# Network two with seven-product steps: four output sums placed singly at the hand-over between passes, weight stores and loads at other slots, last joins on VectorE

## The chip, the cores and the metric

The kernel runs on one core of a Trainium2 chip. The metric is the time of one execution on the device in microseconds (us); less is better. PE is TensorE (matrix products), DVE is VectorE, ACT is ScalarE, POOL is GpSimd, and SP is the queue that issues nearly all DMAs.

## What is computed

Three stages follow each other on 4 x 3072 = 12288 tokens of 256 values, all in float32:

```python
X = np.fft.fft(np.fft.fft(x, axis=1), axis=2).real
xk = mu_k * X + (1.0 - mu_k) * x_prev          # x_prev: the token before
xr = mu_r * X + (1.0 - mu_r) * x_prev
k = np.maximum(xk @ w_k, 0.0)                  # 256 -> 1024
y = 1.0 / (1.0 + np.exp(-(xr @ w_r))) * ((k * k) @ w_v)
h = y @ w_in                                   # 256 -> 2048
out = (h - np.tanh(h)) @ w_out                 # 2048 -> 256
```

The last two lines are network two, the part that the change concerns.

## The kernel before

**Number format.** Every float32 operand of a product is held as two tiles, a rounded high part (cast by ACT, `hi`) and the rest (subtracted by DVE or POOL, `lo`). One product is three matmuls (`mm3`, lines 395 to 397 in the trace): high x high, high x low, low x high. Each moves 512 columns.

**Passes and steps.** The tokens go through in 12 passes of 2 x 512. Network one takes 4 quads of a pass, network two 8 steps, each with 256 of the 2048 hidden units. A step (n, q) is one 2 x 2 block product: the first matrix by seven products after Winograd (`P`), tanh and subtraction on the four blocks, then the second matrix. The four sums of a pass that leave the core are the PSUM tiles `o` (in the code `C[n, t, h]`, t the token half, h the channel half). In pass 0 and in odd steps the second matrix takes eight products that go straight into `o` (`whole`). In even steps of passes 1 to 11 it takes seven (hence "sevens"): three go straight into `o` (`direct`: a12, s4, a22), four go to a bank `k` and are added up in SBUF tiles `acc` (`apart`: a11, s2, s3, s1), since each of them enters several outputs. PE does the second matrix of a step one or two steps later, so the last products of pass n-1 fall into steps (n, 0) and (n, 1).

**The turn.** When pass n-1 is done, `joined` forms the four sums of the `acc` tiles with four additions, in step (n, 0), and `ready` adds each of them to its `o` tile on DVE and issues the store of 256 KB. Both calls of `ready` stand in step (n, 1), and each handles two outputs one behind the other. Ten turns (n = 2 to 11) are of this kind; the turn from pass 0 to pass 1 has no `acc` tiles, and `done` copies the four `o` tiles out.

**What sets the order.** The program is written out by hand: every engine runs its instructions in the order of the code, and waits stand only where data or a buffer are missing. Besides, `at(slot, f)` puts jobs into numbered slots, and each call of `fill()` runs the jobs of one slot. A step has four slots; z0 = 192 is the slot of step (0, 0).

**Weights of network two.** `weights2(slot, q)` loads a block of `w_in` from the DRAM buffer `wf` (line 926), splits it and forms its sums into the tile `TI` (`ti`, ACT and POOL), and four slots later forms the rest (`TI<-t`). `keep` (line 940) stores the finished tile to the DRAM buffer `ti`, from which `stream` (line 1190) reads it back three steps ahead of use in passes 1 to 11. `seven(slot, q)` does the same for the block of `w_out` that an even step needs (`W7`, three loads at line 951, two slots ahead of the first use). The loads of both for the seven-product forms share the one buffer `wf` of pool `p2a`. `left2` loads the next pass's inputs (`xk<-spill`) and forms their sums on POOL.

**Names in the rows.** `x`, `z`, `w`, `k` are PSUM banks of one step, `c` a tanh, `g` a block of h - tanh(h), `m`, `a`, `s` its high and low parts for whole, a and s products. Line 1138 is the addition `z<-w,s` on DVE that frees `w` for the next product; line 1145 subtracts the tanh; line 1068 is ACT's copy `z<-x` at the head of a step, on which PE adds a12.

Of the kernel before, what the change touches and what calls it, by code (L numbers as in the profile page):

```python
# [406 lines left out]
class Kernel:  # L407
# [513 lines left out]
    def weights2(self, slot, q, pool, tag, bufs):  # L921
# [17 lines left out]
        def keep():  # L939
            self.nc.sync.dma_start(out=self.ti[q], in_=out[0].rearrange("p s k n -> p (s k n)").bitcast(F32))  # L940
        self.at(slot, load(a, self.p2a, "wf", 1, 4 + q), ti, None, None, None, lambda: b[0](None))
        self.at(16 * NP + ((5, 6, 10)[q] if q < 3 else 4 * q - 3), keep)
        self.at(slot + 4, load(b, pool, tag, bufs, 12 + q), None, wo)

    def seven(self, slot, q):

        src, t, i = [], [], q // 2
        def load():
            src.append(self.p2a.tile([128, TOK], F32, tag="wf", name="wf", bufs=1) if q else self.kp.tile([128, TOK], F32, tag="xt", name="wf", bufs=4))
            for to, at, n in ((0, 128, 128), (128, 0, 128), (256, 256, 256)):  # L950
                self.nc.sync.dma_start(out=src[0][:, to:to + n], in_=self.wf[12 + q, :, at:at + n])
        def first():
            self.W7[q] = self.p2a.tile([128, 2, 7, 128], F32R, tag=f"TI{i}", name="W7")
            f, g = self.quad_weights(self.p2b, self.W7[q])
            f(src[0])
            t.append(g)
        self.at(slot, load, None, first, None, None, None, lambda: t[0](None))

# [21 lines left out]
    def whole(self, p, blk):  # L980
# [4 lines left out]
        if p["n"] == 0:  # L985
            return self.second(p, blk)
        c = p["w"][int(blk[1]) - 1]
# [30 lines left out]

    def joined(self, n):

        G = self.G
        s1, s2, s3, s5 = (self.acc[n, k] for k in ("a11", "s2", "s3", "s1"))
        G.tensor_add(s2, s2, s1)
        G.tensor_add(s3, s3, s2)
        G.tensor_add(s2, s2, s5)
        G.tensor_add(s5, s5, s3)

    def ready(self, p, t):

        n = p["n"]  # L1030
        if n == 0:
            return
        for h, k in enumerate((("a11", "s2"), ("s3", "s1"))[t]):
            a = self.acc.pop((n, k))
            self.V.tensor_add(a, a, self.C.pop((n, t, h)))
            self.nc.sync.dma_start(out=self.out[n, t, :, h], in_=a)

    def step(self, n, q):
# [30 lines left out]
        if seven:  # L1069
# [6 lines left out]
            P(X, "s2")  # L1076
            late("l12")
            s2 = copied(X)
            t11 = bend(Z)
# [8 lines left out]
            lo("a11", g, G)  # L1088
            add()
            self.fill()  # L1090
            Wb = self.bank("w", "w")
# [6 lines left out]
            if p2 and q == 0:  # L1098
                self.joined(n - 1)
            self.direct(p2, "s4")  # L1100
# [9 lines left out]
        else:  # L1110
# [4 lines left out]
            P(X, "s2")  # L1115
            late("ls1")
            s2 = copied(X)
            t11 = bend(Z)
# [12 lines left out]
            late("hs2", "+s4", "ls2")  # L1131
            if q == 1:
                self.ready(p2, 1)
            self.fill()
# [4 lines left out]
            t22 = bend(Z)  # L1139
            late("hs4", "ls4")  # L1140
            self.fill()
            add()
            if q > 1:
                self.direct(p1, "a12")
            V.tensor_sub(Z, Z, t22)
            hi("22", Z)
            if q == 1:
                self.ready(p2, 0)
            lo("22", Z, V)
# [29 lines left out]
    def phase2(self):  # L1179
# [12 lines left out]
        for g in range(8, 8 * NP):  # L1192
            self.at(z0 + 4 * (g - 3) + 2, lambda g=g: stream(g))
        self.TI = dict(enumerate(self.TI))
        for n in range(NP):
            for q in range(8):
                if n == 0 and q == 1:
                    self.xctx.close()
                    self.p2b = self.ctx.enter_context(self.tc.tile_pool(name="p2b", bufs=1, side="right", reuse_waits="tile"))
                    for j in range(3, 8):  # L1200
                        self.weights2(z0 + 4 * (j - 2), j, self.kp, "xt", 4)
                    for j, slot in ((0, 18), (2, 25), (4, 36), (6, 44)):
                        self.seven(z0 + slot, j)
                if q == 1 and n + 1 < NP:
                    u = self.left2(n + 1)
                    if n == 0:
                        self.at(z0 + 10, u["load"], None, u["a11"], None, u["a12"], None, u["a22"], u["+s1"], u["+s3"], u["+s2"], u["+s4"],
                                u["s1"], None, u["s3"], None, u["s2"], None, u["s4"])
# [8 lines left out]
            if n == 0:  # L1217
                self.pend["over"] = set()
        p, w = self.pend, self.older
        late = lambda *names: [p["late"][k]() for k in names]  # L1220
        late("t21", "c12", "g21", "t12", "h21", "g12", "l21", "h12", "l12")
        self.whole(p, "11")
        add = self.apart(w, "s3")
        self.whole(p, "22")
        add()
        self.direct(w, "s4")
        add = self.apart(w, "s2")
        add()
        self.joined(NP - 1)
        self.whole(p, "21")  # L1230
        self.ready(p, 1)
        self.whole(p, "12")
        self.ready(p, 0)


# [106 lines left out]
```

## Time and profile before

| | us |
|---|---|
| median of 3 runs | 1650.86 (1649.0 to 1650.99) |
| the profiled execution | 1649.88 |
| its span, first to last instruction | 1648.1 |
| PE busy | 1606.5 (97%) |
| DVE, ACT, POOL busy | 1309.6, 1194.2, 1101.5 |
| mean granted TensorE clock | 0.995 of full |

The spectrum takes the first 110 us, network one lasts to 645 us, network two from there to the end. A row of the timeline gives the start, the duration, the engine, the line, the operation with its tiles, and in brackets the idle time of that engine just before it with what ended it. Matmuls are pipelined: a row of 0.39 us starts about 0.23 us behind the one before.

### The profile page before, as it was taken

How to read it: one execution, taken by the hardware profiler on the slowest of the kernel's cores; microseconds unless marked ns; L12 is line 12 of the kernel's file. 1: busy time of each engine (PE TensorE's matmuls, PEld its weight loads, DVE VectorE, ACT ScalarE, POOL GpSimd, SP SyncE). 2: the span in 40 equal slices, each digit the busy share in tenths (PEclk: the TensorE clock that was granted, in tenths of full speed). 3: DMA queues.
4: the chain of work that ended last, by engine and by line, in shares of the span. 5: the costliest groups of instructions: out<-in, count | busy, mean ns of one | idle time of the engine just before them, and what ended most of it. 6: DMA issues, size and time to landing. Idle time of an engine off the chain costs nothing.

```text
span 1648.1 us, 22348 instructions
## 1 busy us (share of the span) xinstructions
PE 1606.5 (97%) x7346; PEld 1322.0 (80%) x7346; DVE 1309.6 (79%) x2023; ACT 1194.2 (72%) x2289; POOL 1101.5 (67%) x913
## 2 busy tenths in 40 slices
PE   8999999999999999989999999999999999999997
PEld 7978888888888887767778787878787878787876
DVE  7987888888898897657777777777777777777776
ACT  5887777777777777767767777777777777777764
POOL 1166667666666666577777768686868686868654
PEclk9999999999999999989999999999999999999999
DMA  9620111011111121544242424242424242414130
GB/s 336 174 58 27 46 46 65 20 45 58 46 65 63 47 90 51 202 156 173 86 139 97 141 90 141 90 141 90 141 90 141 90 146 85 161 69 163 68 116 26
DMA packets 58341, 167.96 MB, mean 102 GB/s; under 512 B 6753, under 2 KB 14945, under 8 KB 58225
## 3 DMA queue, kind: packets, MB, share of 16 engines
q1 hardware_dynamic: 56640, 162.08, 28.6%
q0 software_dynamic: 1440, 4.46, 1.6%
q8 instruction: 58, 0.95, 0.2%
q14 instruction: 59, 0.48, 0.1%
q10 hardware_dynamic: 144, 0.00, 0.0%
HBM read 127.65 MB, written 38.86 MB: 101 GB/s over the span
## 4 chain that ended last, share of the span: by engine, by line
PE 85%; DVE 5%; POOL 3%; ACT 2%; issue 2%; DMA 2%; SPq 1%; POOLq 0%; DVEq 0%; ACTq 0%
PE o L396 11%; PE o L397 11%; PE o L395 11%; PE x L395 7%; PE x L396 7%; PE x L397 7%; PE w L395 4%; PE w L396 4%; PE w L397 4%; PE k L395 2%; PE k L397 2%; PE k L396 2%; PE z L395 2%; PE z L397 2%; PE z L396 2%
## 5 line engine op out<-in xcount | busy, mean ns | idle before, releaser
L1060 POOL TENSOR_TENSOR a<-g,a 128x512 fp32r<-128x512 f32 x132 | 170.4, 1291 | 138.5 <-ACT a L1058 138.0
L696 POOL TENSOR_TENSOR a<-xk,a 128x512 fp32r<-128x512 f32 x70 | 93.2, 1334 | 123.1 <-ACT a L694 123.1
L1060 POOL TENSOR_TENSOR s<-g,s 128x512 fp32r<-128x512 f32 x132 | 170.4, 1295 | 1.0
L395 PE MATMUL o<-m,WO 128*128 128x512 f32 x416 | 162.5, 391 | 0.0
L397 PE MATMUL o<-m,WO 128*128 128x512 f32 x416 | 162.4, 390 | 0.0
L396 PE MATMUL o<-m,WO 128*128 128x512 f32 x416 | 162.4, 390 | 0.0
L696 POOL TENSOR_TENSOR s<-xk,s 128x512 fp32r<-128x512 f32 x94 | 124.8, 1328 | 39.5 <-ACT s L694 36.1
L396 PE MATMUL o<-m,wv 128*128 128x512 f32 x384 | 149.6, 390 | 0.1
L397 PE MATMUL o<-m,wv 128*128 128x512 f32 x384 | 149.5, 389 | 0.0
L395 PE MATMUL o<-m,wv 128*128 128x512 f32 x384 | 149.5, 389 | 0.0
L1050 ACT ACTIVATE c<-z 128x512 f32<-128x512 f32 x176 | 106.6, 606 | 53.2 <-DVE z L1094 31.5
L1167 POOL TENSOR_TENSOR g<-g,g 128x512 f32<-128x512 f32 x88 | 114.0, 1296 | 45.6 <-DVE x L1166 34.7
L1058 ACT CAST a<-g 128x512 fp32r<-128x512 f32 x132 | 82.4, 624 | 58.9 <-DVE g L1104 30.9
L1054 ACT COPY s<-x 128x512 f32<-128x512 f32 x176 | 103.6, 588 | 27.7 <-PE x L397 26.6
L1016 DVE TENSOR_TENSOR acc<-acc,k 128x512 f32<-128x512 f32 x132 | 90.7, 687 | 21.7 <-PE k L397 21.3
L571 ACT ACTIVATE c<-z 128x512 f32<-128x512 f32 x112 | 67.2, 600 | 55.1 <-DVE z L660 54.1
L578 DVE TENSOR_TENSOR m<-z,m 128x512 fp32r<-128x512 f32 x112 | 76.8, 686 | 35.4 <-ACT m L576 35.4
L1058 ACT CAST s<-g 128x512 fp32r<-128x512 f32 x132 | 82.0, 621 | 17.2 <-POOL g L1167 17.0
L430 POOL TENSOR_TENSOR xr<-xt,xr 128x512 fp32r<-128x512 f32 x46 | 60.5, 1322 | 46.6 <-ACT xr L429 46.6
L395 PEld LDWEIGHTS o<-m,WO 128*128 128x128 f32 x416 | 78.4, 188 | 16.5
L397 PEld LDWEIGHTS o<-m,WO 128*128 128x128 f32 x416 | 78.4, 188 | 16.5
L396 PEld LDWEIGHTS o<-m,WO 128*128 128x128 f32 x416 | 78.4, 188 | 16.4
(278 smaller groups left out, 5375.6 us busy)
## 6 DMA issues: line engine op xcount, KB each, us to landing
TI<-ti SPq DMA_DIRECT2D x88, 896.0 KB, 4.8
spill<-r SPq DMA_DIRECT2D x48, 256.0 KB, 2.5
xk<-spill SPq DMA_DIRECT2D x48, 256.0 KB, 6.9
out<-acc SPq DMA_DIRECT2D x44, 256.0 KB
ti<-TI SPq DMA_DIRECT2D x8, 896.0 KB
raw<-w_in SPq DMA_DIRECT2D x32, 128.0 KB, 2.1
cv<-w_out SPq DMA_DIRECT2D x16, 256.0 KB, 3.3
wf<-wf SPq DMA_DIRECT2D x16, 256.0 KB, 3.4
```

The costliest lines, as they stand in the source:

```text
L395: T.matmul(ps, w[0], m[0], start=start, stop=False, skip_group_check=True)
L396: T.matmul(ps, w[0], m[1], start=False, stop=False, skip_group_check=True)
L397: T.matmul(ps, w[1], m[0], start=False, stop=stop, skip_group_check=True)
L571: A.activation(t, src, ACT.Tanh if ph == 2 else ACT.Relu)
L578: V.tensor_sub(M[blk][:, 1], g, M[blk][:, 0].bitcast(F32))
L696: eng.tensor_sub(S[name][:, 1], src(), S[name][:, 0].bitcast(F32))
L1016: self.V.tensor_add(self.acc[key], self.acc[key], K)
L1050: A.activation(t, src, TANH)
L1054: A.copy(t, src)
L1058: A.copy(M[k][:, 0], src)
L1060: eng.tensor_sub(M[k][:, 1], src, M[k][:, 0].bitcast(F32))
L1167: "+s2": lambda: G.tensor_sub(g("22"), g("22"), g("11")), "+s4": lambda: G.tensor_sub(g("12"), g("12"), g("22")),
```

## The change

The turn. `ready` takes one output at a time, and the four calls stand at four places of step (n, 1): (1,0) behind `ls1`, (1,1) behind the copy of the second `k`, (0,0) behind `hi("22")`; (0,1) is first copied from PSUM to SBUF by ACT ("lift", in the place where `hs4` and `ls4` stood) and added in step (n, 2) ("join"). `hs4` and `ls4` of that step move to step (n, 2). The turn from pass 0 to pass 1 uses the same four places with copies. The weights. The loads of `weights2` for `w_in` stand three slots earlier and use the four buffers `xt` of pool `kp`; `keep` of q = 3 to 7 stands four slots later; the loads of `seven` stand five or six slots ahead of the first use, and that use 4 to 7 slots later than before. The inputs of pass 1 are loaded two slots later. The end. The last two seven-products (`s3`, `s2`) stand earlier among PE's work, the joins run on DVE instead of POOL, and the four outputs are placed one by one.

```diff
@@ weights2, seven
-        self.at(slot, load(a, self.p2a, "wf", 1, 4 + q), ti, None, None, None, lambda: b[0](None))
-        self.at(16 * NP + ((5, 6, 10)[q] if q < 3 else 4 * q - 3), keep)
+        self.at(max(slot - 3, 16 * NP - 12), load(a, self.kp, "xt", 4, 4 + q))
+        self.at(slot + 1, ti, None, None, None, lambda: b[0](None))
+        self.at(16 * NP + ((5, 6, 10)[q] if q < 3 else 4 * q + 1), keep)
...
-            src.append(self.p2a.tile([128, TOK], F32, tag="wf", name="wf", bufs=1) if q else self.kp.tile([128, TOK], F32, tag="xt", name="wf", bufs=4))
+            src.append(self.p2a.tile([128, TOK], F32, tag="wf", name="wf", bufs=1))
...
-        self.at(slot, load, None, first, None, None, None, lambda: t[0](None))
+        self.at(slot, first, None, None, None, None, lambda: t[0](None))
+        self.at(slot - (6 if q < 6 else 5), load)
@@ ready
-    def ready(self, p, t):
-
-        n = p["n"]
-        if n == 0:
-            return
-        for h, k in enumerate((("a11", "s2"), ("s3", "s1"))[t]):
-            a = self.acc.pop((n, k))
-            self.V.tensor_add(a, a, self.C.pop((n, t, h)))
+    def ready(self, n, t, h, part=None):
+
+        V, key = self.V, (n, t, h)
+        def send(a):
             self.nc.sync.dma_start(out=self.out[n, t, :, h], in_=a)
+        if part == "lift":
+            if n:
+                self.lifted = self.room(self.act, "s", "s", 3)
+                self.A.copy(self.lifted, self.C.pop(key))
+            else:
+                a = self.room(self.p2b, "acc", "o", 6)
+                self.A.copy(a, self.C.pop(key))
+                send(a)
+        elif n:
+            a = self.acc.pop((n, ("a11", "s2", "s3", "s1")[2 * t + h]))
+            V.tensor_add(a, a, self.lifted if part else self.C.pop(key))
+            send(a)
+        elif not part:
+            a = self.room(self.p2b, "acc", "o", 6)
+            V.tensor_copy(a, self.C.pop(key))
+            send(a)
@@ step, even q
             late("l12")
+            if q == 2:
+                p2["late"]["hs4"]()
+                p2["late"]["ls4"]()
             s2 = copied(X)
...
             add()
+            if q == 2:
+                self.ready(n - 1, 0, 1, "join")
             self.fill()
@@ step, odd q
             late("ls1")
+            if q == 1:
+                self.ready(n - 1, 1, 0)
             s2 = copied(X)
...
             late("hs2", "+s4", "ls2")
-            if q == 1:
-                self.ready(p2, 1)
             self.fill()
...
             t22 = bend(Z)
-            late("hs4", "ls4")
+            if q == 1:
+                self.ready(n - 1, 0, 1, "lift")
+            else:
+                late("hs4", "ls4")
             self.fill()
             add()
+            if q == 1:
+                self.ready(n - 1, 1, 1)
...
             hi("22", Z)
             if q == 1:
-                self.ready(p2, 0)
+                self.ready(n - 1, 0, 0)
             lo("22", Z, V)
@@ phase2
+        for j in range(3, 8):
+            self.weights2(z0 + 4 * (j - 2), j, self.kp, "xt", 4)
+        for j, slot in ((0, 26), (2, 34), (4, 42), (6, 50)):
+            self.seven(z0 + slot, j)
...
-                    for j, slot in ((0, 18), (2, 25), (4, 36), (6, 44)):
-                        self.seven(z0 + slot, j)
...
-                        self.at(z0 + 10, u["load"], None, u["a11"], None, u["a12"], None, u["a22"], u["+s1"], u["+s3"], u["+s2"], u["+s4"],
+                        self.at(z0 + 12, u["load"], None, u["a11"], None, u["a12"], None, u["a22"], u["+s1"], u["+s3"], u["+s2"], u["+s4"],
...
-        late("t21", "c12", "g21", "t12", "h21", "g12", "l21", "h12", "l12")
+        add = self.apart(w, "s3")
+        late("t21", "c12", "g21")
+        add()
+        late("t12")
         self.whole(p, "11")
-        add = self.apart(w, "s3")
+        add = self.apart(w, "s2")
+        late("h21", "g12", "l21", "h12")
+        add()
         self.whole(p, "22")
-        add()
+        self.joined(NP - 1, V)
+        late("l12")
         self.direct(w, "s4")
-        add = self.apart(w, "s2")
-        add()
-        self.joined(NP - 1)
         self.whole(p, "21")
-        self.ready(p, 1)
+        self.ready(p["n"], 1, 0)
+        self.ready(p["n"], 1, 1)
         self.whole(p, "12")
-        self.ready(p, 0)
+        self.ready(p["n"], 0, 0)
+        self.ready(p["n"], 0, 1)
```

DVE, the turn in step (2, 1), before; line 1035 is `ready`, 1014 the copy of a `k` bank, 1138 and 1145 the addition and the subtraction on `z`, 1060 a low part:

```order
L1060 TENSOR_TENSOR s_8369<-x,s_8369 128x512
L1125 TENSOR_TENSOR z<-z,c 128x512
L1014 COPY acc<-k 128x512
L1060 TENSOR_TENSOR m_8399<-z,m_8399 128x512
L1035 TENSOR_TENSOR acc<-acc,o_7668 128x512
L1035 TENSOR_TENSOR acc<-acc,o_7700 128x512
L1138 TENSOR_TENSOR z<-w,s 128x512
L1014 COPY acc<-k 128x512
L1145 TENSOR_TENSOR z<-z,c 128x512
L1035 TENSOR_TENSOR acc<-acc,o_7672 128x512
L1035 TENSOR_TENSOR acc<-acc,o_7676 128x512
L1060 TENSOR_TENSOR m_8441<-z,m_8441 128x512
```

The same place after (1048 is `ready`, 1020 the copy, 1160 and 1172 the addition and the subtraction, 1077 a low part):

```order
L1077 TENSOR_TENSOR s_8369<-x,s_8369 128x512
L1048 TENSOR_TENSOR acc<-acc,o_7657 128x512
L1149 TENSOR_TENSOR z<-z,c 128x512
L1020 COPY acc<-k 128x512
L1077 TENSOR_TENSOR m_8401<-z,m_8401 128x512
L1160 TENSOR_TENSOR z<-w,s 128x512
L1020 COPY acc<-k 128x512
L1048 TENSOR_TENSOR acc<-acc,o_7692 128x512
L1172 TENSOR_TENSOR z<-z,c 128x512
L1048 TENSOR_TENSOR acc<-acc,o_7661 128x512
L1077 TENSOR_TENSOR m_8440<-z,m_8440 128x512
```

The four `ready` additions, two by two around `z<-w,s` and ahead of the last low part, are now three single ones, one of them ahead of `z<-z,c`; the fourth stands in step (2, 2), between the first copy of a `k` bank and the addition on `z`. On ACT the high part of s4 has made room for the copy of an `o` tile in step (2, 1) and stands in step (2, 2) behind the high part of 12.

SP, pass 0, steps 5 to 7, before; line 926 loads a weight block, 951 the block of a seven, 940 stores a `TI` tile, 1190 streams one back:

```order
L926 DMA wf<-wf 128x512 x2
L940 DMA ti<-TI 128x1792
L1190 DMA TI<-ti 128x1792
L926 DMA wf<-wf 128x512
L940 DMA ti<-TI 128x1792
L951 DMA wf<-wf 128x128 x2
L951 DMA wf<-wf 128x256
L1190 DMA TI<-ti 128x1792 x3
```

The same stretch after (952 is the seven's load, 1217 the stream):

```order
L952 DMA wf<-wf 128x128 x2
L952 DMA wf<-wf 128x256
L940 DMA ti<-TI 128x1792
L1217 DMA TI<-ti 128x1792
L926 DMA wf<-wf 128x512
L940 DMA ti<-TI 128x1792
L1217 DMA TI<-ti 128x1792
L952 DMA wf<-wf 128x128 x2
L952 DMA wf<-wf 128x256
L940 DMA ti<-TI 128x1792
L1217 DMA TI<-ti 128x1792 x2
```

The second seven's load stood behind the last but one store of a `TI` tile and ahead of all but one stream; now two streams and the first seven's load are ahead of it, and the last store is behind it.

DVE, the end of the program, before; 1016 adds a `k` bank, 1035 is `ready`:

```order
L1159 TENSOR_TENSOR x<-x,c 128x512
L1173 TENSOR_TENSOR w<-w,c 128x512
L1060 TENSOR_TENSOR m_16072<-x,m_16072 128x512
L1060 TENSOR_TENSOR m_16076<-w,m_16076 128x512
L1016 TENSOR_TENSOR acc<-acc,k 128x512 x2
L1035 TENSOR_TENSOR acc<-acc,o_15526 128x512
L1035 TENSOR_TENSOR acc<-acc,o_15555 128x512
```

The same after (1022 adds a `k` bank, 1028 to 1031 are the joins, 1048 is `ready`):

```order
L1186 TENSOR_TENSOR x<-x,c 128x512
L1022 TENSOR_TENSOR acc<-acc,k 128x512
L1200 TENSOR_TENSOR w<-w,c 128x512
L1077 TENSOR_TENSOR m_16107<-x,m_16107 128x512
L1022 TENSOR_TENSOR acc<-acc,k 128x512
L1028 TENSOR_TENSOR acc<-acc 128x512
L1029 TENSOR_TENSOR acc<-acc 128x512
L1030 TENSOR_TENSOR acc<-acc 128x512
L1031 TENSOR_TENSOR acc<-acc 128x512
L1077 TENSOR_TENSOR m_16111<-w,m_16111 128x512
L1048 TENSOR_TENSOR acc<-acc,o_15541 128x512
```

The additions of the `k` banks stand two and one instructions earlier, the joins have come over from POOL, and the last low part `m<-w` stands behind them.

## Rows read from the trace of the kernel before

**Rows 1.** Windows: stretch, busy us (x instructions) of PE, PEld, DVE, ACT, POOL; clock; DMA.

```profile
729.38:735.36 5.98, 5.97 (x14) 4.68 (x15) 4.43 (x7) 3.69 (x7) 2.80 (x4) 0.52 0.42 173
...
850.00:900.00 50.00, 50.00 (x222) 41.35 (x221) 38.04 (x58) 36.98 (x69) 39.90 (x32) 1.00 0.28 97
900.00:950.00 50.00, 48.64 (x213) 39.63 (x213) 38.93 (x61) 35.78 (x66) 36.62 (x30) 1.00 0.39 134
```

**Rows 2.** Waits of PE: us in total, times, longest.

```profile
PE w L395 <- DVE z L1138: 6.9, 10, 0.7
...
PE z L395 <- ACT z L1068: 6.7, 10, 0.7
```

**Rows 3.** Timeline of PE at the turn of passes 1 and 2 to 3.

```profile
919.93 0.50 PE L395 MATMUL w<-s,TI 128*128 128x512 f32 x1 [0.69 <-DVE z L1138]
...
924.31 0.50 PE L395 MATMUL z<-a,TI 128*128 128x512 f32 x1 [0.68 <-ACT z L1068]
```

**Rows 4.** Timeline of DVE at the same turn.

```profile
916.03 0.70 DVE L1125 TENSOR_TENSOR z<-z,c 128x512 f32<-128x512 f32 x1 [0.81 <-ACT c L1050]
...
917.38 0.69 DVE L1060 TENSOR_TENSOR m<-z,m 128x512 fp32r<-128x512 f32 x1
917.99 1.27 DVE L1035 TENSOR_TENSOR acc<-acc,o 128x512 f32<-128x512 f32 x2
919.18 0.69 DVE L1138 TENSOR_TENSOR z<-w,s 128x512 f32<-128x512 f32 x1
...
921.15 1.27 DVE L1035 TENSOR_TENSOR acc<-acc,o 128x512 f32<-128x512 f32 x2
922.90 0.69 DVE L1060 TENSOR_TENSOR m<-z,m 128x512 fp32r<-128x512 f32 x1 [0.48 <-ACT m L1058]
...
929.45 0.70 DVE L1094 TENSOR_TENSOR z<-w,s 128x512 f32<-128x512 f32 x1 [0.72 <-PE w L397]
```

**Rows 5.** Timeline of ACT at the same turn.

```profile
921.76 0.62 ACT L1058 CAST s<-g 128x512 fp32r<-128x512 f32 x1 [1.26 <-POOL g L1167]
...
923.68 0.57 ACT L1068 COPY z<-x 128x512 f32<-128x512 f32 x1 [0.32 <-DVE m L1060]
```

**Rows 6.** Timelines of POOL, SP, ACT and PE in step (0, 7).

```profile
721.23 1.29 POOL L430 TENSOR_TENSOR TI<-t,TI 128x512 fp32r<-128x512 f32 x1
...
722.55 0.32 SPq L940 DMA_DIRECT2D ti<-TI  x1
722.97 2.15 SPq L951 DMA_DIRECT2D wf<-wf  x3
...
727.33 0.51 ACT L429 CAST W<-wf 128x384 fp32r<-128x384 f32 x1 [6.21 <-DMA wf<-wf]
...
729.38 0.80 PE L395 MATMUL x<-s,TI 128*128 128x512 f32 x1 [6.52 <-ACT s L593]
```

**Rows 7.** Timelines of ACT and PE in steps (0, 4) and (0, 5).

```profile
687.47 0.51 ACT L429 CAST TI<-wf 128x384 fp32r<-128x384 f32 x1 [1.21 <-DMA wf<-wf]
...
690.77 0.50 PE L395 MATMUL z<-a,TI 128*128 128x512 f32 x1 [0.47 <-DVE m L578]
```

**Rows 8.** Timelines of POOL and PE in step (1, 5).

```profile
792.34 1.28 POOL L1060 TENSOR_TENSOR a<-g,a 128x512 fp32r<-128x512 f32 x1
...
793.67 0.50 PE L396 MATMUL o<-a,W 128*128 128x512 f32 x1 [1.17 <-POOL a L1060]
```

**Rows 9.** Timelines of DVE and POOL at the end.

```profile
1636.08 0.69 DVE L1016 TENSOR_TENSOR acc<-acc,k 128x512 f32<-128x512 f32 x1 [1.05 <-PE k L397]
...
1636.85 1.29 POOL L1023 TENSOR_TENSOR acc<-acc 128x512 f32<-128x512 f32 x1 [5.99 <-DVE acc L1016]
...
1642.20 2.48 DVE L1035 TENSOR_TENSOR acc<-acc,o 128x512 f32<-128x512 f32 x4 [5.43 <-POOL acc L1026]
```

**Rows 10.** Timelines of DVE and POOL in step (0, 5).

```profile
701.64 1.33 DVE L687 TENSOR_TENSOR c<-c 128x512 f32<-128x512 f32 x1 [0.15 <-ACT c L571]
...
701.12 1.29 POOL L704 TENSOR_TENSOR xk<-xk 128x512 f32<-128x512 f32 x1
```

More of the change, by code (lines that the diff above doesn't have):

```diff
@@ L985, in whole @@
         if p["n"] == 0:
-            return self.second(p, blk)
+            self.second(p, blk)
+            if p["q"] == 7:
+                t = int(blk[0]) - 1
+                self.C.update({(0, t, h): self.O[t][h] for h in range(2)})
+            return
         c = p["w"][int(blk[1]) - 1]
@@ L1017, in apart, with joined @@
         return add
-    def joined(self, n):
-        G = self.G
+    def joined(self, n, G):
         s1, s2, s3, s5 = (self.acc[n, k] for k in ("a11", "s2", "s3", "s1"))
@@ L1098, in step @@
             if p2 and q == 0:
-                self.joined(n - 1)
+                self.joined(n - 1, G)
             self.direct(p2, "s4")
@@ L1199, in phase2 @@
                     self.p2b = self.ctx.enter_context(self.tc.tile_pool(name="p2b", bufs=1, side="right", reuse_waits="tile"))
-                    for j in range(3, 8):
-                        self.weights2(z0 + 4 * (j - 2), j, self.kp, "xt", 4)
-                    for j, slot in ((0, 18), (2, 25), (4, 36), (6, 44)):
-                        self.seven(z0 + slot, j)
                 if q == 1 and n + 1 < NP:
@@ L1217, in phase2 @@
             if n == 0:
-                self.pend["over"] = set()
+                self.pend.update(over=set(), done=lambda n, t, O: None)
         p, w = self.pend, self.older
         late = lambda *names: [p["late"][k]() for k in names]
-        late("t21", "c12", "g21", "t12", "h21", "g12", "l21", "h12", "l12")
+        add = self.apart(w, "s3")
+        late("t21", "c12", "g21")
+        add()
+        late("t12")
         self.whole(p, "11")
-        add = self.apart(w, "s3")
+        add = self.apart(w, "s2")
+        late("h21", "g12", "l21", "h12")
+        add()
         self.whole(p, "22")
-        add()
+        self.joined(NP - 1, V)
+        late("l12")
         self.direct(w, "s4")
-        add = self.apart(w, "s2")
-        add()
-        self.joined(NP - 1)
         self.whole(p, "21")
-        self.ready(p, 1)
+        self.ready(p["n"], 1, 0)
+        self.ready(p["n"], 1, 1)
         self.whole(p, "12")
-        self.ready(p, 0)
+        self.ready(p["n"], 0, 0)
+        self.ready(p["n"], 0, 1)
     def run(self):
```

## The prediction

> **What bounds the kernel now.** I read the busy time by stretch first. From 850 to 900 us, where no pass ends, PE is busy all 50.00 us and starts 222 matmuls, one per 0.225 us; from 900 to 950, where a pass ends, it is busy 48.64 us and starts 213 [rows 1]. So PE sets the time wherever it doesn't stand, and a change pays only where it stands: the nine missing matmuls are 9 x 0.225 = 2.0 us per turn. The table of PE's waits says that this repeats: ten waits on the addition on `z` of step (n, 1) and ten on ACT's copy into `z` of step (n, 2), 0.7 us each at most [rows 2]. One turn shows both, 0.69 and 0.68 us [rows 3]. Idle time is 1.37 us of the 2.0; the rest is the slow start behind each gap (the first matmul takes 0.50 us). I therefore price a gap of 0.7 us at 1.0, idle plus 0.3.
>
> Three more places stand out. In step (0, 7) PE stands 6.52 us [rows 6], and in the 5.98 us after that it starts only 14 matmuls at a granted clock of 0.52 of full, the lower of the two levels, 1.2 GHz [rows 1]. At 0.225 us they would have taken 3.15, so 2.8 us more are lost; before the fall PE had done nothing for 6.5 us, and the gaps of 0.7 us left the clock alone. At 690.77 and at 793.67 PE stands 0.47 and 1.17 us [rows 7, 8]. And the end is a chain of DVE and POOL alone: the last `k` added at 1636.08, the first of the joins on POOL at 1636.85, `ready` from 1642.20 for 2.48 us [rows 9].
>
> **The turn, ten times.** Before, DVE runs two `ready` additions from 917.99 to 919.26, and `z<-w,s` comes only at 919.18 [rows 4]. PE's last product of the step must wait for it, since it writes into `w`: the gap of 0.69. After, one of these two stands ahead of `z<-z,c`, where DVE is idle for 0.81 us [rows 4] and one addition takes 1.27 / 2 = 0.63: it costs nothing there. The other three come later. `z<-w,s` can follow the low part `m<-z` of 917.38 at 917.99, 1.2 us earlier; the gap closes.
>
> The second gap has another cause. ACT waits 1.26 us for POOL's sum of s4 before it casts `s<-g` at 921.76, and the cast of block 22 stands behind it; so the low part `m<-z` runs at 922.90, and the copy into `z` at 923.68, on which PE waits [rows 3 to 5]. After, this cast stands in step (2, 2), and ACT copies an `o` tile instead, which waits for nothing late and costs about 0.6 us (the copy of 0.57 in rows 5 is of that shape), in the time in which ACT would wait for DVE. The new chain, in DVE's spacing of 0.61 us: `z<-w,s` 917.99, copy of `k` 918.60, `ready` 919.21, `z<-z,c` 919.82 to 920.5, ACT's cast to 921.1 (`ready` (0,0) runs on DVE meanwhile), low part to 921.85, copy into `z` from 921.95 to 922.5. PE, without the two losses of 1.0, would want `z` at 924.31 - 2.0 = 922.3. So about 0.2 us of idle stays, with its slow start 0.4 (idle plus, for so short a stop, a shorter start). Per turn 2.0 - 0.4 = 1.6, for ten 16.0 us. Bounds: 20 if nothing stays, 10 if the second gap stays whole.
>
> What is moved into step (n, 2) must be hidden there. The cast costs ACT 0.6 us; it stands ahead of ACT's copy of `x`, and what waits for that is PE's next product on `x`, behind six matmuls of `whole` 22 and three into `k`: 9 x 0.225 = 2.0 us of cover, less the copy's own 0.6. The join is one DVE addition of 0.7 us ahead of `z<-w,s`, where DVE is idle 0.72 us waiting for PE [rows 4]. If it overruns, the next to notice is PE's product into `w` at the end of the step, behind nine matmuls after the product into `w` that the addition reads, again 2.0 us less the addition itself, so 1.3.
>
> The rule that speaks against this join is a lock. An addition with both inputs in SBUF took 1.33 us instead of 0.69 while POOL was in the middle of an operation of 1.29 [rows 10], and the join is such an addition, where `ready` before had one input in PSUM. So it may take 0.7 to 1.3 us and hold POOL up by as much, inside the cover of 1.3. The Trainium skill, "SBUF — State Buffer", section "SBUF: two separate sides", says the same as an exclusive lock: whichever of a VectorE instruction with two SBUF inputs and a GpSimd instruction starts first has the shared ports for its whole length. By the cover the lock adds nothing to the sum; without it, up to 0.6 us per turn, a rival below.
>
> **The weights.** ACT stood 6.21 us in step (0, 7) for the load of the second seven. SP issued that load at 722.97, only after the store of a `TI` tile at 722.55, and this had waited for POOL to finish the tile at 721.23 + 1.29 = 722.52 [rows 6]. ACT's order put PE's copies behind that cast. After, the store stands four slots later, a whole step behind the making of its tile, and each seven's load is five or six slots ahead of its use. A slot is a quarter of a step of 45 matmuls, 45 x 0.225 / 4 = 2.5 us, so the lead is 12 to 15 us against the 4.4 from issue to cast (722.97 to 727.33). The first seven's piece moves out of the stretch in which POOL was late. What hides the loads if SP is late again: SP has now to pass two streams, which wait until PE is through with an older `TI` buffer. I take the whole wait and the low clock as gained: 6.5 + 2.8 = 9.3. The same goes for 690.77: ACT had waited 1.21 us for a `TI` load issued one slot ahead [rows 7], now four. That is 0.47 + 0.3 = 0.8. Together 10.1; bounds 0 (a stop of the same size elsewhere) and 11.
>
> In pass 1 more of the sevens' pieces fall into the stretch where POOL already makes PE wait (1.17 us at 793.67 for the low part of 792.34, [rows 8]). One piece of 128 x 512 is 1.29 us [rows 6]. At worst one such piece more is ahead, at best the wait of 1.17 + 0.3 goes; the inputs' sums keep their place, so I take half a piece: 0.7 us lost, between -1.5 (gained) and 1.3. The copies at the turn from pass 0 to 1 are as many as before, at other places, and are taken as nothing.
>
> **The end.** PE's product behind the last `k` stands nine matmuls earlier, 2.0 us, so that addition goes from 1636.08 to about 1634.0. The four joins are additions of 0.69 us, each waiting for the one before, 0.8 with the hand-over: to 1637.2, where POOL needed to 1642.1 [rows 9]. POOL is done with its work by then, so no lock. But the last low part `m<-w` stands behind the joins: to 1638.0, and PE's last six matmuls wait for it, with the slow start to about 1639.9; then `ready` of the last two outputs, to 1640.8. Before, DVE's last addition ended at 1642.20 + 2.48 = 1644.7. Gain 3.8 us; bounds 2.5 (the addition of the last `k` no earlier) and 4.5.
>
> **The sum.** 16.0 + 10.1 - 0.7 + 3.8 = 29.2 us. The profiled execution took 1649.88, 1.8 of it outside its span of 1648.1: 1649.9 - 29.2 = 1620.7. The median of the three runs is 1.0 above that execution, which would give 1621.7. I forecast 1621.
>
> **The rivals.**
> 1. The turn closes half: DVE's chain still ends late and the copy into `z` keeps its gap of 1.0. For it: between `z<-w,s` and the copy stand five DVE instructions, as many as before. Against: the cast that waited for POOL is gone from the chain. 10 instead of 16: 1627.
> 2. The stop in step (0, 7) moves to a later weight load, since all sevens now share one buffer and SP stands behind stores and streams. For it: SP's order, in which one late item holds all. Against: leads of 12 us and more. 9.3 us back: 1630.
> 3. The lock, at its full price of 0.6 us per turn, where the cover of 1.3 is used up by DVE being late: 10 x 0.6: 1627. For it: rows 10. The Trainium skill's page "SBUF — State Buffer" states the rule; its cover is this kernel's.
> 4. Everything closes: 4 us more in the turn, 2 in pass 1: 1615.
> 5. Slower. The cast of s4 and its low part on POOL now stand in step (n, 2), one step nearer to PE's product s4. If POOL is late there, PE stands, and a stop long enough drops the clock: 2.0 us of standing plus the 2.8 of low clock seen once, ten times, 48 us: 1649.9 - 29.2 + 48 = 1669. It decides from (29.2 + 3.3) / 10 = 3.3 us per turn. Against: the cast is ACT's fourth instruction behind the copy into `z` at 922.5, 0.6 us each, so it ends about 925, the low part (1.3 us) about 926.3, and PE comes to the product 24 matmuls behind 922.5, at 927.9. POOL would have to be 1.6 us late before PE stands at all, and 4.9 if the clock holds.
>
> **How the numbers follow.** The forecast has 0.62 (on its own 1615 to 1626), rival 1 0.13, rival 2 0.12, rival 3 0.06, rival 4 0.05, rival 5 0.02. A range of 1614 to 1631 leaves out rival 5, the far side of rivals 2 and 4 and the tails of the forecast, some 0.18 in all. A measurement of this kernel can tell 0.2%, 3.3 us, from no change. Every case but rival 5 is far below 1647.6: faster 0.97, same 0.01, slower 0.02.
>
> **What would show it.** Right: PE's table of waits without the ten on the addition on `z`, those on the copy into `z` at 0.3 us or less, or gone; no idle of ACT for a DMA in steps (0, 4) to (1, 4), and a granted clock of 1.00 through pass 0; a stretch of 50 us with a turn that starts 219 to 221 matmuls; DVE's last addition some 3.8 us nearer to the last `z` work. Wrong: a new wait of PE on `o<-s,W` in step (n, 2), on DVE's join, or on a seven's tile; a stretch at the low clock anywhere but at the start and the end; a wait on POOL in pass 1 of over 2.8 us.

## The result, and the profile after

The changed kernel takes **1622.45 us** (median of 4 runs, 1621.86 to 1622.98) against 1650.86 (1649.0 to 1650.99): 28.4 us less, ratio 0.983, 95% interval 0.9813 to 0.9847. The forecast was 1621 with a range of 1614 to 1631. The profiled execution has a span of 1621.2 us.

PE's busy time by stretch, to be read beside [rows 1] (columns: stretch, its length, then for each engine busy us and instructions, the granted clock, DMA share, GB/s):

```profile
700.00:750.00 50.00, 49.60 (x213) 39.25 (x212) 37.23 (x57) 37.62 (x71) 39.31 (x38) 1.00 0.42 144
750.00:800.00 50.00, 47.01 (x201) 37.05 (x200) 35.12 (x54) 36.80 (x70) 44.60 (x42) 1.00 0.41 146
...
850.00:900.00 50.00, 50.00 (x222) 41.35 (x221) 38.55 (x60) 37.16 (x68) 36.72 (x30) 1.00 0.27 93
900.00:950.00 50.00, 49.99 (x220) 40.66 (x219) 40.85 (x62) 37.01 (x69) 42.96 (x35) 1.00 0.40 135
```

The stretch with a turn now starts 220 matmuls instead of 213, two short of the undisturbed 222. In these rows the granted clock is 1.00, its higher level; the stop of step (0, 7) is gone. The poorest stretch of network two, but for the end, is now 750 to 800, in pass 1, with 201 matmuls and POOL busy for 44.60 of 50 us.

PE's waits from 640 to 1640 us, without the shortest (us in total, times, longest); the twenty of [rows 2] are not among them:

```profile
PE o L396 <- POOL a L1077: 2.5, 2, 1.3
PE k L395 <- ACT m L1075: 0.7, 1, 0.7
...
PE z L395 <- ACT z L1085: 0.4, 1, 0.4
...
```

One turn, the same as in [rows 3 to 5]: DVE, ACT and PE in step (n, 1) and at the start of (n, 2) (start in us, duration, engine, line, operation, out<-in; in brackets the idle time ahead and what ended it):

```profile
909.65 0.70 DVE L1160 TENSOR_TENSOR z<-w,s 128x512 f32<-128x512 f32 x1
910.25 0.68 DVE L1020 COPY acc<-k 128x512 f32<-128x512 f32 x1
910.85 0.68 DVE L1048 TENSOR_TENSOR acc<-acc,o 128x512 f32<-128x512 f32 x1
911.45 0.69 DVE L1172 TENSOR_TENSOR z<-z,c 128x512 f32<-128x512 f32 x1
912.05 0.68 DVE L1048 TENSOR_TENSOR acc<-acc,o 128x512 f32<-128x512 f32 x1
912.79 0.69 DVE L1077 TENSOR_TENSOR m<-z,m 128x512 fp32r<-128x512 f32 x1
...
912.17 0.59 ACT L1075 CAST m<-z 128x512 fp32r<-128x512 f32 x1 [0.72 <-DVE z L1172]
913.57 0.57 ACT L1085 COPY z<-x 128x512 f32<-128x512 f32 x1 [0.31 <-DVE m L1077]
...
912.37 0.40 PE L397 MATMUL o<-a,W 128*128 128x512 f32 x1
912.78 0.50 PE L395 MATMUL o<-m,WO 128*128 128x512 f32 x1
913.12 0.39 PE L396 MATMUL o<-m,WO 128*128 128x512 f32 x1
914.28 0.41 PE L395 MATMUL z<-a,TI 128*128 128x512 f32 x1
```

ACT waits for DVE now, no longer for POOL. The copy into `z` ends at 914.14, and PE's matmul on `z` starts at 914.28 unhindered. What is left stands one product earlier: the matmul of 912.78 starts 0.41 us behind the one before it, the next 0.34, where 0.227 is usual: 0.18 + 0.11 = 0.29 us. It waits for the addition of 912.05, which empties its `o` bank; the idle time of PE is 0.01 us here and at most 0.04 in the other turns. The last section says why so little idle time goes with so late a start.

**Where the time went.** PE runs the same 7346 matmuls in every kernel here, in the same order but for two products near the end, so matmul by matmul the start in one trace can be taken from that in another. Gained (+) or lost (-) against the kernel before, by stretches of its time, in us:

| kernel | to 685 | 685 to 741: weights of pass 0 | 741 to 833: pass 1 | 833 to 1593: ten turns | from 1593: the end |
|---|---|---|---|---|---|
| changed | -1.2 | +10.8 | -2.6 | +15.7 | +4.1 |
| e1_turn | -0.3 | +1.4 | -1.0 | +15.2 | 0.0 |
| e2_weights | -0.2 | +10.8 | -1.4 | +0.7 | 0.0 |
| e3_end | -0.7 | +1.1 | 0.0 | +0.2 | +4.1 |
| e4_cast_back | -0.3 | +10.8 | -2.7 | +0.9 | +4.1 |
| e5_store | -3.5 | +10.4 | -0.1 | +0.4 | 0.0 |
| e11_store_only | -1.4 | +10.3 | -1.3 | +15.5 | +4.1 |
| e13_best_slots | -3.6 | +10.3 | +0.7 | +15.6 | +4.1 |

In the first stretch the changes show nothing: between 600 us, ahead of all of them, and 685 us no kernel gains or loses 0.1 us. What stands in the column differs from execution to execution; the last section says by what. So 28.0 us of the changed kernel's gain is its own: 10.8 - 2.6 + 15.7 + 4.1.

### The profile page after: what moved, and what is told of

The parts are those of the page before. It is cut to its first block, busy times and chain, and to the rows that moved or that the text cites. A ratio compares the mean times of both kernels' runs of the same rounds, so it can differ in the third digit from the quotient of the medians.

```text
span 1621.2 us, 22373 instructions
## 1 busy us (share of the span) xinstructions
PE 1602.8 (99%) x7346; PEld 1320.0 (81%) x7346; DVE 1315.5 (81%) x2028; ACT 1196.1 (74%) x2298; POOL 1103.2 (68%) x909
## 3 DMA queue, kind: packets, MB, share of 16 engines
q1 hardware_dynamic: 56640, 162.08, 29.2%
## 4 chain that ended last, share of the span: by engine, by line
PE 92%; POOL 2%; DVE 2%; DMA 2%; issue 1%; ACT 1%; SPq 0%; DVEq 0%; POOLq 0%; ACTq 0%
PE o L395 13%; PE o L396 12%; PE o L397 12%; PE x L395 8%; PE x L397 8%; PE x L396 8%; PE w L395 4%; PE w L397 4%; PE w L396 4%; PE k L395 2%; PE k L396 2%; PE k L397 2%; PE z L395 2%; PE z L397 2%; PE z L396 2%; PE r L396 1%
## 5 line engine op out<-in xcount | busy, mean ns | idle before, releaser
L1077 POOL TENSOR_TENSOR a<-g,a 128x512 fp32r<-128x512 f32 x132 | 175.5, 1329 | 130.3 <-ACT a L1075 129.8
L1194 POOL TENSOR_TENSOR g<-g,g 128x512 f32<-128x512 f32 x88 | 114.2, 1298 | 38.7 <-DVE x L1193 29.2
L576 ACT CAST m<-z 128x512 fp32r<-128x512 f32 x112 | 65.8, 587 | 28.7 <-DVE z L664 22.7
```

The costliest lines, as they stand in the source:

```text
L1077: eng.tensor_sub(M[k][:, 1], src, M[k][:, 0].bitcast(F32))
L1194: "+s2": lambda: G.tensor_sub(g("22"), g("22"), g("11")), "+s4": lambda: G.tensor_sub(g("12"), g("12"), g("22")),
```

## The experiments

**One part alone, three times.** The edits are the three parts of the change, each on the kernel before.

> The kernel before with the turn alone changed (the four sums placed one by one, the cast of s4 and its low part in step (n, 2)); weights, loads, stores and the end as before. Theory: each of the ten turns gives back 1.5 to 1.6 us as in the changed kernel, 15.6 in all: 1635.3. The stop of 6.5 us in step (0, 7) stays. Pass 1 loses nothing, since no piece of a seven moves. Rival (the turn from pass 0 to pass 1, which the prediction took as nothing, is what cost 2.6 us in pass 1): 1637.9, with the new waits of PE between steps (1, 0) and (1, 5).

> The kernel before with the weights' loads and stores alone changed; turn and end as before. Theory: 1.3 us come back at the TI load of step (0, 4), 9.6 at the stop of step (0, 7), and 2.6 are lost in pass 1, where the sevens' first pieces now stand on POOL ahead of two low parts that PE waits for: 1650.9 - 8.3 = 1642.6, with two waits of PE of over 1 us on a low part from POOL. Rival (pass 1 loses by the turn, not by the weights): 1640.0 and no such waits.

> The kernel before with the end alone changed (PE's last k product earlier, joins on VectorE). Theory: 4.2 us, 1646.7; DVE's last addition follows PE's last product within 1 us. Rival: the joins are hidden wherever they stand and only PE's earlier product pays, 2.0 us: 1648.9.

| kernel | us | ratio to before, 95% interval | gain |
|---|---|---|---|
| e1_turn | 1635.62 | 0.9912 (0.9899 to 0.9926) | 14.8 |
| e2_weights | 1640.29 | 0.9942 (0.9926 to 0.9957) | 10.2 |
| e3_end | 1645.94 | 0.9974 (0.9966 to 0.9983) | 4.5 |

The kernel before took 1650.44 beside them. The three gains add up to 29.5, the change as a whole brought 28.4: the parts hardly meet. Of the two theories on pass 1 neither is right alone. The turn loses 1.0 us there without any moved piece, the weights lose 1.4 without the turn, together 2.4 of the 2.6. PE waits for a low part from POOL once in e1_turn, for 1.2 us, but so it does in the kernel before [rows 8]: the 1.0 us of e1_turn are not in it. They are late starts of 0.2 us at `w` and 0.3 at `o` in step (1, 1), of 0.2 at 771.37 and of 0.4 at 780.69, with 0.4 won back at 751.74; the rest is in smaller ones. The waits on a low part from POOL in e2_weights:

```profile
PE o L396 <- POOL a L1062: 1.6, 2, 1.3
```

In the changed kernel they are two as well, 2.5 us in all, but the first of them has grown from 0.26 to 1.17 us: it needs both parts. What is ahead of it on POOL, and PE's stop:

```profile
758.92 1.02 POOL L430 TENSOR_TENSOR W<-wf,W 128x384 fp32r<-128x384 f32 x1 [0.23 <-ACT W L429]
759.90 0.46 POOL L516 TENSOR_TENSOR t<-wf 128x128 f32<-128x128 f32 x1
...
761.70 1.30 POOL L696 TENSOR_TENSOR a<-xk,a 128x512 fp32r<-128x512 f32 x1
762.95 1.28 POOL L1077 TENSOR_TENSOR a<-g,a 128x512 fp32r<-128x512 f32 x1
...
764.28 0.50 PE L396 MATMUL o<-a,W 128*128 128x512 f32 x1 [1.17 <-POOL a L1077]
```

A seven's first piece is a 128x384 low part and four sums of 128x128: from 758.92 to 761.70 it holds POOL for 2.8 us, and the low part that PE waits for stands behind it. That is the share of the weights. The share of the turn comes over SP:

```profile
748.15 0.34 SPq L1037 DMA_DIRECT2D out<-o  x1
...
749.01 2.16 SPq L916 DMA_DIRECT2D xk<-spill  x4
...
755.46 0.62 ACT L694 CAST a<-xk 128x512 fp32r<-128x512 f32 x1 [1.14 <-DMA xk<-spill]
```

The same cast in e2_weights:

```profile
752.74 0.62 ACT L694 CAST a<-xk 128x512 fp32r<-128x512 f32 x1 [0.23 <-DMA xk<-spill]
```

The store of the output that ACT now copies in step (1, 1) stands ahead of the loads of the next pass's inputs, and these go out at 749.01, against 745.53 in e2_weights, where PE is no more than 1.1 us further at that place. So ACT waits 1.14 us for them instead of 0.23, and POOL begins its row of work later. The two differences are equal, 0.91 us at ACT and 0.91 at PE's stop. All kernels here with the turn changed have this wait of ACT, 0.75 to 1.65 us; the four without have 0 to 0.33. This share is read from the traces; no run moves that load alone.

**Which edit closes the turn.**

```diff
-            if q == 2:
-                p2["late"]["hs4"]()
-                p2["late"]["ls4"]()
...
             if q == 1:
                 self.ready(n - 1, 0, 1, "lift")
-            else:
-                late("hs4", "ls4")
+            late("hs4", "ls4")
```

> The changed kernel with the cast of s4 and its low part back in step (n, 1), behind ACT's copy of the o tile and ahead of the cast of block 22. Theory of the prediction (the second gap came from this cast, which waits for POOL's sum): PE's wait on the copy into z comes back in each of the ten turns, 0.7 to 1.6 us idle and 0.3 of slow start, 10 to 19 us in all: 1632 to 1641; the first gap stays closed. Rival (the gap closed because the ready additions left the chain on DVE): no wait comes back, 1622 to 1624.

Measured: 1638.02 us, ratio to before 0.9925 (0.9912 to 0.9939), 15.6 us above the changed kernel. PE's waits in it, from 640 to 1640 us:

```profile
PE z L395 <- ACT z L1085: 13.7, 11, 1.3
```

ACT in one turn of it:

```profile
913.93 0.62 ACT L1075 CAST s<-g 128x512 fp32r<-128x512 f32 x1 [1.77 <-POOL g L1190]
914.46 0.58 ACT L1075 CAST m<-z 128x512 fp32r<-128x512 f32 x1
```

The cause that the prediction names is shown: with the cast of s4 back, ACT waits 1.77 us for POOL's sum, the cast of block 22 stands behind it, and the second gap is back in each turn. But it is back at 1.33 us, twice what it was, while the first gap stays closed: of the ten turns' 15.7 us only 0.9 are left. The two gaps were not two prices. PE's arrival at the second was set by the first; with the first alone closed PE arrives earlier and waits longer for the same late copy. In this kernel the `ready` additions and the copy by ACT stand as in the changed one, so the first gap closes by them alone; the cast moved alone, with the additions where they were, was not run.

**Store or lead.** The change moves both SP's stores of the `TI` tiles and the loads of the sevens.

```diff
-        self.at(16 * NP + ((5, 6, 10)[q] if q < 3 else 4 * q - 3), keep)
+        self.at(16 * NP + ((5, 6, 10)[q] if q < 3 else 4 * q + 1), keep)
```

> The kernel before with one edit: the store of each TI tile four slots later. The loads of the sevens stay where they were, two slots ahead of their use. Theory of the prediction (the load of the second seven stood behind a store that waited for POOL): with the store gone from there the load needs 4.4 us from issue to cast and has two slots, 5 us; the stop of step (0, 7) goes, 8 to 9.6 us: 1641 to 1643. Rival (it is the short lead that makes ACT wait, whoever stands ahead on SP): the stop shrinks by the wait of the store alone and PE still stands some us there: 1645 to 1649.

This edit undone in the changed kernel is the other experiment:

> The changed kernel with the stores of the TI tiles back at their old slots; the loads keep their new lead. Theory: a lead of five or six slots is itself enough, since each load is issued before the store that waits: no stop, within 1 us of the changed kernel, 1621.5 to 1623.5. Rival 2 of the prediction (one late item on SP holds all behind it, whatever the lead): a stop comes back in or near step (0, 7), 5 to 10 us: 1627 to 1632.

Measured: e5_store 1639.96 us (0.9934, 0.9919 to 0.9949), 11.3 below before; e6_old_store 1623.12 (0.9828, 0.9813 to 0.9842), as the changed kernel. Either edit alone removes the whole stop. SP and ACT in e5_store, to be read beside [rows 6]:

```profile
717.89 1.27 SPq L951 DMA_DIRECT2D wf<-wf  x3
...
724.17 0.32 SPq L940 DMA_DIRECT2D ti<-TI  x1
...
721.43 0.52 ACT L429 CAST W<-wf 128x384 fp32r<-128x384 f32 x1
```

The load goes out at 717.89 with no store that waits in front of it, and ACT casts it at 721.43 without idling. The same edit also frees the place at 690.77 us: e5_store gains 1.2 us there, as the changed kernel does. What stood on SP there in the kernel before, and what it waited for on POOL:

```profile
674.88 1.29 POOL L430 TENSOR_TENSOR TI<-t,TI 128x512 fp32r<-128x512 f32 x1 [6.96 <-ACT TI L429]
...
676.19 2.47 SPq L940 DMA_DIRECT2D ti<-TI  x2
...
681.51 0.97 SPq L926 DMA_DIRECT2D wf<-wf  x2
```

The two stores go out when POOL is done, at 676.17, then four loads of inputs, and only then the two weight loads; ACT's cast of 687.47 in [rows 7] waits for the second of them, which lands 5.3 us after its issue. So the store is a cause there too, and the short lead is one only together with it: e6_old_store, with the stores at their old slots and the new leads, gains the same 1.2 us at this place.

**What moving the sevens costs.** First their pieces as early as their tiles allow:

```diff
-        for j, slot in ((0, 26), (2, 34), (4, 42), (6, 50)):
+        for j, slot in ((0, 10), (2, 16), (4, 22), (6, 28)):
```

> The changed kernel with the sevens' pieces at slots 10, 16, 22 and 28 of network two instead of 26, 34, 42 and 50, their loads ahead by as much. Theory (what pass 1 lost is POOL's lateness behind the sevens' first pieces, one of 1.02 and four of 0.46 us): POOL is busy only half of the time from 650 to 700 us, so the pieces are hidden there; PE's waits on a low part from POOL at 764 and 786 us go, 2 to 3.5 us: 1619 to 1620.5. Rival (the pieces then delay the weights of pass 0, or their loads stand ahead of others): no gain or a new wait of PE between 660 and 740 us: 1622 to 1627.

Measured: 1629.13 us (0.9864, 0.9847 to 0.988), 6.7 above the changed kernel. Pass 1 gains 1.25 us against the kernel before, so what pass 1 lost does hang on these pieces; but the rival holds in pass 0, where PE stands 2.51 and 4.96 us. PE's waits in it:

```profile
PE z L395 <- DVE m L578: 7.5, 2, 5.0
```

ACT ahead of the longer one:

```profile
728.57 0.62 ACT L429 CAST WO<-wf 128x512 fp32r<-128x512 f32 x1 [6.52 <-DMA wf<-wf]
```

ACT waits 6.52 us for a weight load that SP issued only at 725.16, behind the load of a seven at 723.85; and this had waited for the sevens' one buffer, which POOL left with the last sum of the piece before at 723.81. Then the other way, the loads and pieces back where the kernel before had them, with the store alone moved:

> The changed kernel with the loads and pieces of the weights and of the second pass's inputs back as in the kernel before; only the stores of the TI tiles stay four slots later. Theory: the later store alone frees both places of pass 0, and the sevens' pieces at their old slots spare pass 1 the 1.4 us that moving them cost beside the turn: 1621. Rival (the leads of the loads are what holds pass 0 together once the turn is changed): a wait for a load in pass 0, 1624 or more.

Measured: 1621.84 us (0.9822, 0.9809 to 0.9836). Pass 1 loses 1.3 instead of 2.6 us, and no weight load is late; only the inputs' load is, by 1.40 us, as in the other kernels with the turn changed. Against the changed kernel that is 0.6 us, within the intervals.

**The rest of the turn.** Two attempts on the 0.29 us at the `o` bank. The first puts the copy of `k` last:

```diff
             self.fill()
-            add()
+            if q != 1:
+                add()
             if q == 1:
                 self.ready(n - 1, 1, 1)
...
             if q == 1:
                 self.ready(n - 1, 0, 0)
+                add()
```

> The changed kernel with one move: at the turn, DVE's copy of k in step (n, 1) stands behind the last of the output additions instead of ahead of the second one. In the changed kernel each turn still loses 0.3 us where PE's product into an o bank waits for the addition that empties it. Theory (that addition is late only by DVE's queue): it comes up to 0.6 us earlier, the 0.3 go, ten times: 1619.5. Rival (the next wait, on the copy into z, is as late as this one: it ended 0.14 us ahead of PE's need): 0.1 us per turn at most: 1621.5 to 1622.5.

Measured: 1637.48 us (0.9915, 0.99 to 0.993), 15.0 above the changed kernel. Neither theory saw it: the bank that this copy empties is the one into which PE writes its next `x`. PE's waits in it:

```profile
PE x L395 <- DVE acc L1020: 17.4, 11, 1.6
```

DVE and PE in one turn of it:

```profile
914.38 0.68 DVE L1020 COPY acc<-k 128x512 f32<-128x512 f32 x1
...
915.12 0.50 PE L395 MATMUL x<-a,TI 128*128 128x512 f32 x1 [1.57 <-DVE acc L1020]
```

The second exchanges two additions on DVE:

```diff
-                self.ready(n - 1, 1, 1)
+                self.ready(n - 1, 0, 0)
...
-                self.ready(n - 1, 0, 0)
+                self.ready(n - 1, 1, 1)
```

> The changed kernel with two of the output additions of step (n, 1) in each other's place: (0, 0) where (1, 1) stood, one addition and one z<-z,c earlier on DVE, and (1, 1) where (0, 0) stood. Nothing else moves on DVE. Theory: PE's product into the bank of (0, 0), the one that still waits at each turn, is free of it, and the bank of (1, 1) is asked for only some ten matmuls later; 0.29 us come back ten times, 2.9 in all: 1619.5. Rival (the copy into z, 0.14 us ahead of PE's need, becomes the next wait): 1.4 at most: 1621.

Measured: 1622.99 us (0.983, 0.9816 to 0.9843), no gain. The wait at the bank is gone, and the copy into `z` has taken its place, at the full price (ACT and PE in one turn):

```profile
913.77 0.57 ACT L1085 COPY z<-x 128x512 f32<-128x512 f32 x1 [0.31 <-DVE m L1077]
...
913.92 0.39 PE L397 MATMUL o<-m,WO 128*128 128x512 f32 x1
914.39 0.50 PE L395 MATMUL z<-a,TI 128*128 128x512 f32 x1
```

The matmul of 914.39 starts 0.47 us behind the one before it, and the next 0.33: 0.25 + 0.11 lost, against 0.29. The chain to this copy is what bounds the turn now.

**Together.** The exchange and the store alone, and then also the last two sevens a step earlier (slots 31 and 37 for 36 and 44):

> e10 and e11 in one kernel. Theory: the two gains add up, 2.9 + 1.4: 1618. Rival (both take away the same wait): 1619.5.

> As the kernel before it in this call, with the last two sevens' pieces at slots 31 and 37 instead of 36 and 44. Theory: POOL's lateness at 787 us, the last wait of over 1 us, comes from these pieces, and a step earlier POOL has room: 1616.5. Rival (they collide there with the inputs' pieces, as the early slots did at 693 and 730 us): 1618 to 1624.

Measured: 1621.77 (0.9822, 0.9809 to 0.9835) and 1620.19 us (0.9816, 0.9802 to 0.9829). In e12_best neither expectation came: the exchange, which gained nothing alone, adds nothing here, and the ten turns gain 15.5 us with it as without. The last is the lowest median here, 2.3 below the changed kernel, with PE's wait on POOL in pass 1 gone (+0.7 us in the table instead of -2.6). The two intervals overlap, so that it is faster than the changed kernel is not shown by the times; that pass 1 no longer loses is shown by its trace. By the table, without the first column, it gains 30.7 us against 28.0.

## Why the prediction was right, point by point

- **The turn: 16.0 forecast, 15.7 measured.** Both causes are as named, and the size of what stays is near: 0.4 per turn forecast, 20.0 - 15.7 over ten turns measured, 0.3 of it at one place. That place was off by one product: `z` comes 0.14 us in time, and the last addition frees its `o` bank too late. e10_swap shows the two within 0.1 us of each other. The lower bound, 10 if the second gap stays whole, was wrong: e4_cast_back has just that case, and it gains 0.9. The step that failed here is the pricing of the two gaps as independent terms of 1.0, when the second grows by what the first gives back; the sum came right only because both closed.
- **Step (n, 2) hides what is moved there.** The cast is at 916.03 and its low part ends on POOL at 918.02, PE's product on it starts at 919.80: 1.8 us of margin, 1.6 forecast. So rival 5 was far. The join met the lock of [rows 10] in nine of ten turns:

```profile
918.23 1.29 POOL L696 TENSOR_TENSOR a<-xk,a 128x512 fp32r<-128x512 f32 x1 [0.20 <-ACT a L694]
...
918.88 1.19 DVE L1048 TENSOR_TENSOR acc<-acc,s 128x512 f32<-128x512 f32 x1
919.99 0.69 DVE L1116 TENSOR_TENSOR z<-w,s 128x512 f32<-128x512 f32 x1
...
919.47 1.75 POOL L1077 TENSOR_TENSOR a<-g,a 128x512 fp32r<-128x512 f32 x1
...
921.86 0.39 PE L395 MATMUL w<-s,TI 128*128 128x512 f32 x1
```

  It took 1.19 us instead of 0.68, and POOL's next operation 1.75 instead of 1.29. `z<-w,s` behind it is still done at 920.68, 1.18 us ahead of the product into `w`. Rival 3's price is real, its cover held. The Trainium skill, "SBUF — State Buffer", section "SBUF: two separate sides", has the lock go to whichever of the two instructions starts first, for its whole length. These rows agree: each of the two took 0.5 us longer.
- **The weights: 10.1 forecast, 10.8 measured.** 9.5 in step (0, 7) for 9.3, and 1.2 at 690.77 for 0.8. The reading of SP in step (0, 7) was right. At 690.77 the prediction saw the short lead alone, and not the stores ahead of the load; the longer lead frees the place all the same (e6_old_store). Rival 2 (one late item on SP holds all) did not win in pass 0, since the later store and the longer lead each remove the stop alone. But its mechanism acts in pass 1, at a smaller price, where the turn's own store holds the loads of the inputs.
- **Pass 1: -0.7 forecast, between +1.5 and -1.3; measured -2.6.** This is the term that was mis-sized, outside its own bounds, in two steps. A seven's piece was priced at 1.29 us, the price of its second part, when its first part holds POOL for 2.8 us; the trace of before has these rows too, at other times. And the turn from pass 0 to pass 1, whose copies were "taken as nothing", costs this stretch 1.0 us without the weights (e1_turn), and with them it adds most of the wait of 1.17 us. A sign that the prediction gave for being right failed by it: between steps (0, 4) and (1, 4) ACT does idle for a DMA once, the 1.14 us at 755.46.
- **The end: 3.8 forecast, 4.1 measured.** The last `k` is added at 1611.21 in the changed kernel, which is 1634.0 on the time axis of before (22.75 us had been gained by then), as forecast. The joins take 0.73 each instead of 0.8:

```profile
1611.21 0.69 DVE L1022 TENSOR_TENSOR acc<-acc,k 128x512 f32<-128x512 f32 x1
1611.94 0.69 DVE L1028 TENSOR_TENSOR acc<-acc 128x512 f32<-128x512 f32 x1
...
1614.72 0.68 DVE L1077 TENSOR_TENSOR m<-w,m 128x512 fp32r<-128x512 f32 x1
1615.32 2.47 DVE L1048 TENSOR_TENSOR acc<-acc,o 128x512 f32<-128x512 f32 x4
```

  PE's last products wait 0.64 us for the low part of 1614.72, but the `ready` additions start before PE is through and end at 1617.79: the end is DVE's chain alone, and the low part's place in it costs no more than its own 0.6.

In all 29.2 forecast and 28.0 measured, with errors of -0.3 (turn), +0.7 (weights), -1.9 (pass 1) and +0.3 (end), which partly cancel: that the total is this near is in part luck.

## What to carry to other kernels

Two waits of one engine for the same chain of work are not two prices: close the first alone and the second grows by as much, so follow the chain to the last late link (here a cast that waited for another engine's sum) and price the whole. On a queue that works in order, ask of every late transfer what stood in front of it before blaming its lead: a store that waits for its data holds all loads behind it, and one that the change itself puts there does so too. And when work is moved on an engine, count all of its instructions at the new place, not the one that is easiest to see, above all in a stretch where that engine is 90% busy.

## What the runs showed of the hardware

**The lock can be lost several times in a row.** In network one DVE runs an operation on one SBUF input (line 452, on `cva`), 0.42 us mostly, that meets a row of POOL operations. In e13_best_slots it took 3.64 us. DVE and POOL there:

```profile
227.91 3.64 DVE L452 TENSOR_SCALAR cva<-cva 128x512 f32<-128x512 f32 x1
...
227.48 1.30 POOL L707 TENSOR_TENSOR xk<-xk 128x512 f32<-128x512 f32 x1
228.72 1.30 POOL L696 TENSOR_TENSOR s<-xk,s 128x512 fp32r<-128x512 f32 x1
229.97 1.30 POOL L430 TENSOR_TENSOR xr<-xt,xr 128x512 fp32r<-128x512 f32 x1
```

DVE is done only when POOL has nothing more to do, and POOL's operations keep their 1.30 us. In the changed kernel the same instruction took 1.15 us and POOL's next one 1.48 instead of 1.30: there DVE came in between. The two cases look alike as long as DVE waits; its start lay 0.43 us behind that of POOL's operation in one and 0.42 in the other. In this execution PE then stood 1.59 us, at 233.55, on a product that DVE's queue held up; e5_store has the same at 372.44, for 1.60 us, with 3.66 us for the operation. Matmul by matmul, each costs 1.9 of the 3.6 and 3.5 us in the table's first column. So a collision, which the prediction priced at 1.3 us at most for its join, can cost DVE three of POOL's operations; the ten joins themselves took 1.19 us at most.

**The clock of the spectrum differs between executions.** From 20 to 60 us the granted clock is 0.96 in the traces of the changed kernel, e5_store, e11_store_only and e13_best_slots, and 1.00 in those of the kernel before and of e1 to e4. The first four lose 1.1 to 1.2 us between 30 and 60 us, the others nothing: this is the other large part of the first column. What lowers the clock there was not followed.

**A stop of 0.01 us costs 0.29.** The matmul behind a stop starts later than the idle time tells, and the second another 0.11 us late: at 912.78 above, where PE is idle for 0.01 us, 0.18 and 0.11; at 914.39 in e10_swap, where it is idle for 0.09, 0.25 and 0.11. The first part follows from the rows: one of 0.39 us starts 0.23 behind the one before, so two rows overlap by 0.16, and a start that is late by no more than that shows as no idle time at all. A list of idle times alone would not have shown the 0.3 us that a turn still loses at its `o` bank.

**The low clock behind the stop of step (0, 7) did not last equally long.** The stop itself was 6.52 us in the kernel before, 6.44 in e1_turn and 6.38 in e3_end. In the 5.98 us from the first matmul behind it they started 14, 19 and 20 matmuls at a granted clock of 0.52, 0.71 and 0.76, and up to 741 us e1_turn and e3_end lost 1.1 and 1.3 us less than the kernel before. The stops of 1.17 and 1.32 us in the changed kernel left the clock at 1.00.
